# The last 64 rows of the query projection as row pairs, six tiles to a PSUM bank

## The chip, the cores and the metric

The kernel runs on one core of a Trainium2 chip. The metric is the device time of one execution in microseconds, the median of several. TensorE (PE in the profile) multiplies; VectorE (DVE) and ScalarE (ACT) move its results from PSUM to SBUF and do the softmax; GpSimd (POOL) and SyncE (SP) do little here.

## The reference

Four layers, each added to its input: a recurrent memory attention A, a gated unit B, and both once more with the same weights. A goes through 64 segments of 32 tokens one after the other. Each takes 8 memory rows from the segment before.

```python
for s in range(n_seg):                      # 64 segments of 32 tokens
    h = jnp.concatenate([mem, xs], axis=1)  # 8 + 32 rows of 448
    q, k, v = h @ Wq, h @ Wk, h @ Wv        # 16 heads of 256
    p = _softmax(where(mask, q @ k.T * scale, -1e9))
    o = (p @ v) @ Wo
    mem = o[:, :M, :].copy()
    outs.append(o[:, M:, :])
# B: h = relu(x @ W_gate) * (x @ W_up); h @ W_down, with F = 1792
```

(Einsums are written as products here.) Both layers see their input after a layer norm.

## The kernel before

**Fused weights.** For each head the kernel multiplies Wq with the transposed Wk once, at the start (`fuse_qk`), and Wv with Wo (`fuse_vo`). A head is then one 448 x 448 matrix each, in `A_sb` and `B_sb`. The query projection of a step is h times the matrices in `A_sb`, and its result goes straight against h.

**Dimensions.** 448 is three blocks of 128 and one of 64. In `A_sb` the index kd = 0 to 3 is the block of contracted rows; for kd = 3 only the lower 64 rows hold data, and the upper 64 are zero (the memset at line 135). The columns of 16 heads make 2 halves (hf) of 28 tiles of 128 (`NT`): 24 whole tiles, and 4 in which the last 64 columns of two heads stand together.

**Two chains.** The two A layers run interleaved, the second four segments behind the first (`LAG`), so that 60 of the 68 steps work on two segments at once: 2 x 40 = 80 moving columns. The 8 steps at the ends have one chain and 40 columns. Every second step also carries a block of 64 rows of each layer's B (`Feed`: residual, norm, xposed, gate_up, down, norm2, feed_on, leave).

**A step** issues, on TensorE in exactly the order of the program (`in_order`):
- `project`: for each group u of 4 tiles, 16 matmuls `prj` into one bank of PSUM, then a cast to `TQ` by DVE or ACT in turn (the group 6 goes to `TZ` by both). For the first half the groups 6, 0 to 5, then `hk_make` (transposes `kps`), then the same for the second half
- `scores_m(0)`, in between the groups of the second half: the memory scores `Sm`, and on DVE and ACT their softmax (mx, se, ssum, rs, PM)
- behind the projection `flipped(PM[0])` (transposes `pps`), `scores_x` (`Sx`), `weigh_m` (`ya`, `yb`), `scores_m(1)` and `scores_x(1)`
- `project_out` (`ox`), with the gated unit (`ups`, `gps`, `dps`) between its parts in every second step, `project_tail` (`o`), `weigh_m_rows` (`ym`) and `weigh_x` (`y`); the last of these, the weighting of the second half, ends the step

The order on DVE and ACT is set when the program is built. All results of TensorE but `ox` take turns in seven PSUM buffers (pool `psum`). A matmul can use 64 rows of the array alone; `gate_up` issues such matmuls in turn for the lower rows (`ups`) and the upper ones (`gps`). `weigh_x` and `weigh_m_rows` do so with 40 rows.

The code of before, with the profile's line numbers:

Of the kernel before, what the change touches and what calls it, by code (L numbers as in the profile page):

```python
# [8 lines left out]
BF = mybir.dt.bfloat16  # L9
# [43 lines left out]
def build_kernel(ctx, tc, A_x, A_mem0, A_Wq, A_Wk, A_Wv, A_Wo, B_W_gate, B_W_up, B_W_down, out,  # L53
# [26 lines left out]
    def mm(*a, **k):  # L80
        in_order(nc.tensor.matmul(*a, **k))  # L81
# [4 lines left out]
    def evac(eng, dst, src):  # L86
        if eng is nc.scalar:
            nc.scalar.copy(dst, src)  # L88
        else:
            eng.tensor_copy(dst, src)  # L90
# [40 lines left out]
    half = glob.tile([P, 1], F32, name="half")  # L131
    nc.vector.memset(half[:], -0.5)

    A_sb = glob.tile([P, 4, 2, NT, 128], BF, name="A_sb")
    nc.gpsimd.memset(A_sb[ROWS[1], 3], 0.0)
    B_sb = glob.tile([P, 2, NT, DM], BF, name="B_sb")

    hTb = []
# [57 lines left out]
    with tc.tile_pool(name="pre", bufs=3) as pre:  # L196
# [37 lines left out]
        def dims(t, r, e, c, n=1):  # L234
            o = 64 * c if r == 0 else DM + 64 * ((c + 1) % NPASS)
            return t[:, e, o:o + 64 * n]

        def halves(dst, lhs, rhs):
            for t in range(2):
                for eo in range(2):  # L240
                    mm(dst[ROWS[eo]], lhs(eo, 2 * eo + t), rhs(2 * eo + t), start=(t == 0), stop=(t == 1),
                       tile_position=(0, 64 * eo))

        def fuse_qk(p, qk):
            hf, p4 = divmod(p, 4)
            mx_ps = psum.tile([P, 4, 128], F32, tag="ps", name="mxw")
            for kd in range(4):
                rows = slice(0, P if kd < 3 else 64)
                for eo in range(2):
                    aps = psum.tile([P, 3, 128], F32, tag="ps", name="aps")  # L250
                    for t in range(2):
                        e = 2 * eo + t
                        mm(aps[:, :, :], qk[:, e, kd * 128:kd * 128 + 128], dims(qk, 1, e, 0, 6),
                           start=(t == 0), stop=(t == 1))
                    for t in range(2):
                        e = 2 * eo + t
                        mm(mx_ps[:, kd, eo * 64:eo * 64 + 64], qk[:, e, kd * 128:kd * 128 + 128], dims(qk, 1, e, 6),
                           start=(t == 0), stop=(t == 1))
                    evac(nc.scalar if eo or kd == 2 else nc.vector,
                         A_sb[rows, kd, hf, eo * 4 + p4:eo * 4 + p4 + 17:8, :], aps[rows])  # L260
            evac(nc.vector, A_sb[:, 0:3, hf, 24 + p4, :], mx_ps[:, 0:3])
            evac(nc.scalar, A_sb[ROWS[0], 3, hf, 24 + p4, :], mx_ps[ROWS[0], 3])

        def fuse_vo(p, vv, wo):
            hf, p4 = divmod(p, 4)
# [110 lines left out]
    class Feed:  # L376


        def __init__(self, i):
            self.i = i  # L380
            self.first = i < nblk
            self.second = 0 <= i - LAG // BLK < nblk
            self.n = slice(0 if self.second else TB, P if self.first else TB)
            self.x = xa[i % 3]
            self.nx = xp[i % 2]
# [60 lines left out]
                rows_in(nc.scalar, self.i + 2, 0, tps[:, :, 0:TB])  # L446


    def moving(hb, j, idx, chains):

        if len(chains) == 2:
            return hb[:, j, idx * HI:(idx + 1) * HI].rearrange("p (c k) -> p c k", k=64)[:, :, 0:L]
        c = chains[0]
        return hb[:, j, idx * HI + 64 * c:idx * HI + 64 * c + L]

    def project(hf, chains, hb, j, us):

        n = L * len(chains)
        for u in us:
            ps = psum.tile([P, 512], F32, tag="ps", name="prj")  # L460
            for p4 in range(4):
                for kd in range(4):
                    mm(ps[:, p4 * n:(p4 + 1) * n], A_sb[:, kd, hf, 4 * u + p4, :],
                       moving(hb, j, kd, chains), start=(kd == 0), stop=(kd == 3))
            if u < 6:
                parts = [(nc.scalar if u % 2 else nc.vector, slice(0, P), TQ[hf][:, :, u, :])]
            else:
                parts = [(nc.vector, slice(0, 64), TZ[hf][0:64, :, 0:64]),
                         (nc.scalar, slice(64, 128), TZ[hf][64:128, :, 64:128])]
            for eng, rows, T in parts:  # L470
                T = T.rearrange("p g (t q) -> p t g q", q=16)
                if len(chains) == 2:
                    evac(eng, T, ps[rows, 0:4 * n].rearrange("p (t g q) -> p t g q", t=4, q=16))
                    continue
                c = chains[0]
                src = ps[rows, 0:4 * n].rearrange("p (t w) -> p t w", t=4)
                x, m = (0, SEG) if c == 0 else (MEM, 0)
                evac(eng, T[:, :, 2, MEM * c:MEM * c + MEM], src[:, :, m:m + MEM])
                evac(eng, T[:, :, 3 * c:3 * c + 2, :],
                     src[:, :, x:x + SEG].rearrange("p t (g q) -> p t g q", q=16))  # L480

    def queries(hf, g, kd):
        return TQ[hf][:, g, 2 * kd:2 * kd + 2, :] if kd < 3 else TZ[hf][:, g, :]
# [49 lines left out]
    def step(g, ff):  # L533
# [12 lines left out]
        def hk_make():  # L546
            kps = psum.tile([P, 4, 128], BF, tag="ps", name="kps")
            for i in range(4):
                tr(kps[:, i, :], hb[:, j, i * HI:(i + 1) * HI], ident[:])
            hk = HK[g % 2]  # L550
            nc.vector.tensor_copy(hk[:, 0:4, :], kps[:])
            nc.scalar.copy(hk[:].rearrange("p k n -> p (k n)")[:, 512:768].rearrange("p (a b) -> p a b", b=64)[:, 0::3, :],
                           kps[:, 3, :].rearrange("p (a b) -> p a b", b=64))
            return hk

        def scores_m(hf):
            if not ms:
                return
            Sp = psum.tile([P, 2, L], F32, tag="ps", name="Sm")
            for kd in range(4):  # L560
                mm(Sp[:, :, :], queries(hf, 2, kd), moving(hb, j, kd, (0, 1)), start=(kd == 0), stop=(kd == 3))
            weights_of(Sp, 2, PM[hf], blk[:], f"m{hf}")

        def scores_x(hf):
            Sp = psum.tile([P, 4, L], F32, tag="ps", name="Sx")
            mm(Sp[:, :, :], ident[:], maskS[:], start=True, stop=False, skip_group_check=True)
            for half in range(2):
                for c in chains:
                    for kd in range(4):
                        mm(Sp[:, 2 * half + c, :], queries(hf, 3 * c + half, kd), moving(hb, j, kd, (c,)),  # L570
                           start=False, stop=(half == 1 and c == chains[-1] and kd == 3), skip_group_check=True)
            return Sp
# [4 lines left out]
        def weigh_m(hf, hk, PT):  # L577
            if not ms:
                return
            ya = psum.tile([P, 256], F32, tag="ps", name="ya")  # L580
            for kd in range(2):
                mm(ya[:, kd * 128:kd * 128 + 128], hk[:, kd, :], PT[:], start=True, stop=True)
            nc.vector.tensor_copy(ys(hf)[:, 0:16, M0:M0 + 16], ya[:].rearrange("p (t q) -> p t q", q=16))  # L583
            yb = psum.tile([P, 192], F32, tag="ps", name="yb")
            mm(yb[:, 0:128], hk[:, 2, :], PT[:], start=True, stop=True)
            for eo in range(2):
                mm(yb[:, 128:192], hk[:, 4 + eo, :], PT[:, 64 * eo:64 * eo + 64], start=(eo == 0), stop=(eo == 1))
            nc.scalar.copy(ys(hf)[:, 16:28, M0:M0 + 16], yb[:].rearrange("p (t q) -> p t q", q=16))
# [89 lines left out]
        def load_some():  # L678
            if g < 3:
                for part in (2 * at[0], 2 * at[0] + 1):  # L680
                    if part < NPASS + FT // 2:
                        load_ff(part)
                at[0] += 1
# [6 lines left out]
            return  # L690

        load_some()
        project(0, chains, hb, j, (6, 0, 1))
        if ff is not None:
            ff.residual()
        project(0, chains, hb, j, (2, 3, 4, 5))
        load_some()
        hk = hk_make()
        if ff is not None:
            ff.norm()  # L700
        project(1, chains, hb, j, (6, 0, 1))
        scores_m(0)
        project(1, chains, hb, j, (2, 3))
        if ff is not None:
            ff.xposed()
        project(1, chains, hb, j, (4, 5))
        if len(chains) == 2:
            pm = flipped(PM[0], 1, "m0")
            Sx0 = scores_x(0)
            weigh_m(0, hk, pm)  # L710
            scores_m(1)
            Sx1 = scores_x(1)
            probs_x(0, Sx0)
        else:
            Sx0 = scores_x(0)
            scores_m(1)
            Sx1 = scores_x(1)
            pm = flipped(PM[0], 1, "m0")
            weigh_m(0, hk, pm)
            probs_x(0, Sx0)  # L720
# [117 lines left out]
```

## Time and profile before

| what | us |
|---|---|
| median of 3 runs (lowest, highest) | 1646.31 (1643.99, 1646.62) |
| the profiled execution | 1647.19 |
| its span in the profile | 1645.4 |
| PE busy / DVE busy / ACT busy in the span | 1614.9 / 1195.1 / 757.6 |
| matmuls prj, 80 columns: count in the trace, busy | 13440, 520.3 |
| casts TQ of 320 elements on DVE: count, busy | 360, 174.2 |
| casts TQ of 320 elements on ACT: count, busy | 360, 153.1 |

A matmul's duration in the profile (about 0.2 us) is that from its issue to its last result; the next one starts much earlier, so the pace is read from one start to the next. Matmuls and weight loads are recorded under line 81, transposes under line 84, copies by ACT under line 88 and by DVE under line 90, since helpers there issue them; the tile's name tells them apart. The granted clock of TensorE is 1.00 in the steps with two chains.

### The profile page before, as it was taken

How to read it: one execution, taken by the hardware profiler on the slowest of the kernel's cores; microseconds unless marked ns; L12 is line 12 of the kernel's file. 1: busy time of each engine (PE TensorE's matmuls, PEld its weight loads, DVE VectorE, ACT ScalarE, POOL GpSimd, SP SyncE). 2: the span in 40 equal slices, each digit the busy share in tenths (PEclk: the TensorE clock that was granted, in tenths of full speed). 3: DMA queues.
4: the chain of work that ended last, by engine and by line, in shares of the span. 5: the costliest groups of instructions: out<-in, count | busy, mean ns of one | idle time of the engine just before them, and what ended most of it. 6: DMA issues, size and time to landing. Idle time of an engine off the chain costs nothing.

```text
span 1645.4 us, 96970 instructions
## 1 busy us (share of the span) xinstructions
PE 1614.9 (98%) x44476; PEld 1495.1 (91%) x44476; DVE 1195.1 (73%) x4095; ACT 757.6 (46%) x2315; POOL 76.7 (5%) x157
## 2 busy tenths in 40 slices
PE   8999999999999999999999999999999999999997
PEld 7688899999999999999999999999999999999985
DVE  7866777777777777777777777777777777777772
ACT  5634444544444444544444444544444444544441
POOL 3100000000000000000000000000000000000000
PEclk9989999999999999999999999999999999999997
DMA  9430000000000000000000000000000000000000
GB/s 267 129 95 8 8 10 8 6 9 9 9 10 10 9 10 8 5 9 9 10 9 9 9 10 8 6 9 9 10 9 10 10 9 8 5 8 6 7 7 6
DMA packets 29465, 33.06 MB, mean 20 GB/s; under 512 B 3320, under 2 KB 28160, under 8 KB 29056
## 3 DMA queue, kind: packets, MB, share of 16 engines
q1 hardware_dynamic: 28992, 26.85, 6.2%
q8 instruction: 348, 5.70, 1.5%
q14 instruction: 61, 0.50, 0.1%
q0 software_dynamic: 64, 0.01, 0.0%
HBM read 23.18 MB, written 1.84 MB: 15 GB/s over the span
## 4 chain that ended last, share of the span: by engine, by line
PE 91%; DVE 5%; ACT 3%; issue 1%; DMA 0%; POOL 0%; POOLq 0%; DVEq 0%; ACTq 0%
PE prj L81 29%; PE ox L81 24%; PE ups L81 10%; PE dps L81 6%; PE o L81 5%; PE y L81 4%; PE Sx L81 3%; ACT xT L401 2%; PE aps L81 1%; PE bps L81 1%; PE Sm L81 1%; DVE TQ L90 1%; PE tpw L84 1%; PE gps L81 1%; PE pps L84 1%; PE kps L84 1%
## 5 line engine op out<-in xcount | busy, mean ns | idle before, releaser
L81 PE MATMUL prj<-hT,A_sb 128*128 128x80 bf16 (+1 forms) x15232 | 571.0, 199 | 0.2
L81 PEld LDWEIGHTS <-A_sb 128*128 128x128 bf16 x15232 | 546.3, 100 | 15.0 <-issue 8.0
L81 PEld LDWEIGHTS <-B_sb 128*128 128x128 bf16 (+1 forms) x15456 | 497.6, 103 | 27.5 <-issue 19.8
L88 ACT CAST TQ<-prj 128x320 bf16<-128x320 f32 (+1 forms) x456 | 170.4, 384 | 120.3 <-PE prj L81 114.3
L81 PE MATMUL ox<-Y,B_sb 128*128 128x80 bf16 (+4 forms) x5880 | 223.2, 199 | 1.9 <-DVE Y L583 1.9
L81 PE MATMUL ox<-Z,B_sb 128*128 128x80 bf16 (+2 forms) x5712 | 217.9, 199 | 1.3 <-DVE Z L583 1.3
L90 DVE CAST TQ<-prj 128x320 bf16<-128x320 f32 (+1 forms) x456 | 192.6, 430 | 29.2 <-PE prj L81 22.2
L81 PE MATMUL gps<-xT,Wgu_sb 64*128 64x128 bf16 (+1 forms) x3332 | 192.8, 215 | 2.6 <-issue 2.4
L81 PE MATMUL ups<-xT,Wgu_sb 64*128 64x128 bf16 (+1 forms) x3332 | 192.8, 215 | 2.2 <-issue 1.3
L81 PEld LDWEIGHTS <-Wgu_sb 64*128 64x128 bf16 x6664 | 180.9, 95 | 7.7 <-issue 5.6
L415 DVE SCALAR_TENSOR_TENSOR hh<-gps,ut 128x256 bf16<-128x256 f32 (+1 forms) x238 | 96.8, 407 | 58.4 <-ACT ut L414 45.8
L414 ACT CAST ut<-ups 128x256 bf16<-128x256 f32 (+1 forms) x238 | 85.6, 360 | 87.5 <-PE gps L81 69.8
L494 ACT ACTIVATE se<-se 128x80 f32<-128x80 f32 (+1 forms) x270 | 74.9, 299 | 105.2 <-DVE se L493 81.3
L88 ACT CAST Y<-y 64x128 bf16<-64x128 f32 (+2 forms) x256 | 89.3, 379 | 45.7 <-DVE Y L90 42.0
L90 DVE CAST Y<-y 64x128 bf16<-64x128 f32 (+2 forms) x256 | 102.1, 419 | 10.9 <-ACT Y L88 2.0
L512 DVE COPY PT<-pps 128x128 bf16<-128x128 bf16 (+1 forms) x206 | 49.8, 256 | 81.0 <-PE pps L84 76.0
L90 DVE CAST Z<-y 64x128 bf16<-64x128 f32 (+2 forms) x256 | 99.1, 418 | 10.2 <-ACT Z L88 3.4
L88 ACT COPY hT<-tps 128x256 bf16<-128x256 bf16 x32 | 11.9, 372 | 195.5 <-DVE hT L90 195.5
L88 ACT CAST Z<-y 64x128 bf16<-64x128 f32 (+2 forms) x256 | 89.2, 378 | 24.0 <-DVE Z L90 17.4
L81 PE MATMUL dps<-Wd_sb,hh 128*128 128x448 bf16 x476 | 98.5, 360 | 0.0
L81 PEld LDWEIGHTS <-TQ 128*128 128x128 bf16 x1938 | 88.3, 97 | 11.2 <-ACT TQ L88 10.8
L88 ACT CAST TZ<-prj 64x320 bf16<-64x320 f32 (+2 forms) x152 | 56.0, 378 | 71.7 <-DVE TZ L90 71.2
(121 smaller groups left out, 2075.6 us busy)
## 6 DMA issues: line engine op xcount, KB each, us to landing
wo<-in_A_Wo_dram SPq DMA_DIRECT2D x8, 448.0 KB, 7.8
nat<-in_A_Wq_dram SPq DMA_DIRECT2D x8, 384.0 KB, 6.0
nat<-in_A_Wk_dram SPq DMA_DIRECT2D x8, 384.0 KB, 6.1
nat<-in_A_Wv_dram SPq DMA_DIRECT2D x8, 384.0 KB, 7.8
xa<-in_A_x_dram SPq DMA_DIRECT2D x32, 56.0 KB, 2.2
xa<-xp SPq DMA_DIRECT2D x32, 56.0 KB, 1.9
out_dram<-xa SPq DMA_DIRECT2D x32, 56.0 KB, 2.0
xp<-in_A_x_dram SPq DMA_DIRECT2D x30, 56.0 KB, 2.1
```

The costliest lines, as they stand in the source:

```text
L81: in_order(nc.tensor.matmul(*a, **k))
L84: in_order(nc.tensor.transpose(*a))
L88: nc.scalar.copy(dst, src)
L90: eng.tensor_copy(dst, src)
L401: nc.scalar.copy(xT[ROWS[r], 4:NPASS, :], tps[ROWS[1 - r], 0:3, :])
L414: nc.scalar.copy(ut[:, :, n], ups[:, :, n])
L415: nc.vector.scalar_tensor_tensor(out=hh[:, 2 * u:2 * u + 2, n], in0=gps[:, :, n], scalar=0.0, in1=ut[:, :, n], op0=ALU.max, op1=ALU.mult)
L494: nc.scalar.activation(se[:], se[:], AF.Exp, scale=SCALE)
L512: nc.vector.tensor_copy(PT[:], pps[:].rearrange("p b q -> p (b q)"))
```

## The change

The rows of kd = 3 leave `A_sb` and go to `A3` and `A3z`, each tile in 64 rows, half of the tiles in the lower and half in the upper ones. A tile's projection is now one matmul of 64 rows and three of 128. The banks hold six tiles (four for `TZ`), so a step has four banks and one `TZ` bank for each half. `open_banks` issues the matmuls of 64 rows for two banks in turn, one on the lower rows, one on the upper ones; `close_bank` adds the three others and casts. A step has three such groups: of 6 pairs at its start, of 10 pairs (with the `TZ` banks of both halves), and of 12 pairs for the second half. A cast has 480 elements. `xposed` moves from inside the projection to behind `weigh_m(0)`, and `scores_m(0)` stands behind the first of the four banks of the second half. `fuse_qk` makes the new tiles with matmuls of 64 columns.

```diff
-    A_sb = glob.tile([P, 4, 2, NT, 128], BF, name="A_sb")
-    nc.gpsimd.memset(A_sb[ROWS[1], 3], 0.0)
+    A_sb = glob.tile([P, 3, 2, NT, 128], BF, name="A_sb")
+    A3 = glob.tile([P, 2, 12, 128], BF, name="A3")
+    A3z = glob.tile([P, 4, 128], BF, name="A3z")
...
-            for kd in range(4):
-                rows = slice(0, P if kd < 3 else 64)
+            for kd in range(3):
...
+            aps = psum.tile([P, 3, 128], F32, tag="ps", name="aps")
+            halves(aps, lambda eo, e: qk[:, e, 384:448], lambda e: dims(qk, 1, e, 0, 6))
+            for eo in range(2):
+                for t in range(2):
+                    e = 2 * eo + t
+                    mm(mx_ps[ROWS[hf], 3, eo * 64:eo * 64 + 64], qk[:, e, 384:448], dims(qk, 1, e, 6),
+                       start=(t == 0), stop=(t == 1), tile_position=(0, 64 * hf))
+            evac(nc.scalar, A3[:, hf, p4:p4 + 9:4, :], aps[:])
             evac(nc.vector, A_sb[:, 0:3, hf, 24 + p4, :], mx_ps[:, 0:3])
-            evac(nc.scalar, A_sb[ROWS[0], 3, hf, 24 + p4, :], mx_ps[ROWS[0], 3])
+            evac(nc.scalar, A3z[ROWS[hf], p4, :], mx_ps[ROWS[hf], 3])
...
-    def project(hf, chains, hb, j, us):
+    class Bank:
+        def __init__(self, hf, i):
+            self.hf = hf
+            self.i = i
+            self.tiles = [tidx(kd, i // 2, 2 * (i % 2) + k) for kd in range(3) for k in range(2)] if i < 4 else list(range(24, NT))
+            self.ps = psum.tile([P, 512], F32, tag="ps", name="prj")
...
+    def open_banks(chains, hb, j, *which):
+        n = L * len(chains)
+        banks = [Bank(hf, i) for hf, i in which]
+        for a, b in zip(banks[::2], banks[1::2]):
+            for k in range(len(a.tiles)):
+                for bk in (a, b):
+                    t = bk.tiles[k]
+                    r, w = last_rows(bk.hf, t)
+                    mm(bk.out(t, n), w, moving(hb, j, 3, chains, ROWS[r]), start=(k == 0), stop=False,
+                       skip_group_check=True)
+        return banks
+
+    def close_bank(bk, chains, hb, j, eng):
+        n = L * len(chains)
+        hf, N = bk.hf, len(bk.tiles)
+        for t in bk.tiles:
+            for kd in range(3):
+                mm(bk.out(t, n), A_sb[:, kd, hf, t, :], moving(hb, j, kd, chains), start=False, stop=(kd == 2),
+                   skip_group_check=True)
...
-        project(0, chains, hb, j, (6, 0, 1))
+        b0, b2 = open_banks(chains, hb, j, (0, 0), (0, 2))
+        close_bank(b0, chains, hb, j, nc.vector)
+        close_bank(b2, chains, hb, j, nc.scalar)
         if ff is not None:
             ff.residual()
-        project(0, chains, hb, j, (2, 3, 4, 5))
+        b1, b3, z0, z1 = open_banks(chains, hb, j, (0, 1), (0, 3), (0, 4), (1, 4))
+        close_bank(b1, chains, hb, j, nc.vector)
         load_some()
+        close_bank(b3, chains, hb, j, nc.scalar)
+        close_bank(z0, chains, hb, j, None)
         hk = hk_make()
         if ff is not None:
             ff.norm()
-        project(1, chains, hb, j, (6, 0, 1))
+        close_bank(z1, chains, hb, j, None)
+        c0, c2, c1, c3 = open_banks(chains, hb, j, (1, 0), (1, 2), (1, 1), (1, 3))
+        close_bank(c0, chains, hb, j, nc.vector)
         scores_m(0)
-        project(1, chains, hb, j, (2, 3))
-        if ff is not None:
-            ff.xposed()
-        project(1, chains, hb, j, (4, 5))
+        close_bank(c2, chains, hb, j, nc.scalar)
+        close_bank(c1, chains, hb, j, nc.vector)
+        close_bank(c3, chains, hb, j, nc.scalar)
         if len(chains) == 2:
             pm = flipped(PM[0], 1, "m0")
             Sx0 = scores_x(0)
             weigh_m(0, hk, pm)
+            if ff is not None:
+                ff.xposed()
             scores_m(1)
```

In the steps with one chain `xposed` stands behind `scores_x(0)`.

More of the change, by code (lines that the diff above doesn't have):

```diff
@@ L259, in fuse_qk @@
                     evac(nc.scalar if eo or kd == 2 else nc.vector,
-                         A_sb[rows, kd, hf, eo * 4 + p4:eo * 4 + p4 + 17:8, :], aps[rows])
+                         A_sb[:, kd, hf, eo * 4 + p4:eo * 4 + p4 + 17:8, :], aps[:])
+            aps = psum.tile([P, 3, 128], F32, tag="ps", name="aps")
[6 more added lines that the diff above has]
+            evac(nc.scalar, A3[:, hf, p4:p4 + 9:4, :], aps[:])
             evac(nc.vector, A_sb[:, 0:3, hf, 24 + p4, :], mx_ps[:, 0:3])
-            evac(nc.scalar, A_sb[ROWS[0], 3, hf, 24 + p4, :], mx_ps[ROWS[0], 3])
+            evac(nc.scalar, A3z[ROWS[hf], p4, :], mx_ps[ROWS[hf], 3])
         def fuse_vo(p, vv, wo):
@@ L446, in feed_on, with moving @@
                 rows_in(nc.scalar, self.i + 2, 0, tps[:, :, 0:TB])
-    def moving(hb, j, idx, chains):
+    def moving(hb, j, idx, chains, rows=slice(0, P)):
         if len(chains) == 2:
-            return hb[:, j, idx * HI:(idx + 1) * HI].rearrange("p (c k) -> p c k", k=64)[:, :, 0:L]
+            return hb[rows, j, idx * HI:(idx + 1) * HI].rearrange("p (c k) -> p c k", k=64)[:, :, 0:L]
         c = chains[0]
-        return hb[:, j, idx * HI + 64 * c:idx * HI + 64 * c + L]
-    def project(hf, chains, hb, j, us):
-        n = L * len(chains)
[L459 to L480, printed above, removed]
@@ new lines, in moving, with out @@
+        return hb[rows, j, idx * HI + 64 * c:idx * HI + 64 * c + L]
+    class Bank:
[4 more added lines that the diff above has]
+            self.ps = psum.tile([P, 512], F32, tag="ps", name="prj")
+        def out(self, t, n):
+            k = self.tiles.index(t)
+            return self.ps[:, k * n:(k + 1) * n]
@@ new lines, in last_rows @@
+    def last_rows(hf, t):
+        if t >= 24:
+            return hf, A3z[ROWS[hf], t - 24, :]
+        kd, eo, p4 = t // 8, t // 4 % 2, t % 4
+        return eo, A3[ROWS[eo], hf, 4 * kd + p4, :]
+    def open_banks(chains, hb, j, *which):
+        n = L * len(chains)
+        banks = [Bank(hf, i) for hf, i in which]
[7 more added lines that the diff above has]
+        return banks
@@ new lines, in close_bank @@
+    def close_bank(bk, chains, hb, j, eng):
[5 more added lines that the diff above has]
+                   skip_group_check=True)
+        ps = bk.ps
+        if bk.i < 4:
+            at = 2 * (bk.i // 2) + bk.i % 2
+            parts = [(eng, slice(0, P), TQ[hf][:].rearrange("p g (k b) w -> p g k (b w)", b=2)[:, :, :, 32 * at:32 * at + 32], 3)]
+        else:
+            parts = [(nc.vector, slice(0, 64), TZ[hf][0:64, :, 0:64].unsqueeze(2), 1),
+                     (nc.scalar, slice(64, 128), TZ[hf][64:128, :, 64:128].unsqueeze(2), 1)]
+        for eng, rows, T, K in parts:
+            T = T.rearrange("p g k (t q) -> p k t g q", q=16)
+            if len(chains) == 2:
+                evac(eng, T, ps[rows, 0:N * n].rearrange("p (k t g q) -> p k t g q", k=K, t=N // K, q=16))
+                continue
+            c = chains[0]
+            src = ps[rows, 0:N * n].rearrange("p (k t w) -> p k t w", k=K, t=N // K)
+            x, m = (0, SEG) if c == 0 else (MEM, 0)
+            evac(eng, T[:, :, :, 2, MEM * c:MEM * c + MEM], src[:, :, :, m:m + MEM])
+            evac(eng, T[:, :, :, 3 * c:3 * c + 2, :],
+                 src[:, :, :, x:x + SEG].rearrange("p k t (g q) -> p k t g q", q=16))
@@ L715, in step @@
             Sx0 = scores_x(0)
+            if ff is not None:
+                ff.xposed()
             scores_m(1)
```

## The prediction

> **What bounds the kernel now.** I read the page first, then the groups of instructions kept apart by shape, then the timeline of one step and of TensorE's changes of array shape, last the windows around the few stretches in which the clock fell.
>
> ```profile
> PE 1614.9 (98%) x44476; PEld 1495.1 (91%) x44476; DVE 1195.1 (73%) x4095; ACT 757.6 (46%) x2315; POOL 76.7 (5%) x157
> ...
> PE 91%; DVE 5%; ACT 3%; issue 1%; DMA 0%; POOL 0%; POOLq 0%; DVEq 0%; ACTq 0%
> ```
>
> TensorE (PE) is busy throughout and is 91% of the chain that ended last. So what the change takes from TensorE's stream counts in full, and so does every wait that it puts into it. DMA is 0% of the chain. The chain in order of time prices the projection:
>
> ```profile
> 803.87 2.29 PE prj L81 x64
> ```
>
> 64 matmuls in 2.29 us are 35.8 ns each (128 rows, 80 columns). The 224 of a step cost 8.02 us; 60 of the 68 steps have both chains, thus 80 columns.
>
> Two more prices come from timelines. The first column is the start, the second the time to the end of the last; matmuls overlap, so I go from start to start.
>
> ```profile
> 827.62 0.42 PE L81 MATMUL ox<-Z,B_sb 128*128 128x80 bf16 x7
> 827.96 0.23 PE L81 MATMUL ups<-xT,Wgu_sb 64*128 64x128 bf16 x1
> 827.97 0.23 PE L81 MATMUL gps<-xT,Wgu_sb 64*128 64x128 bf16 x1
> 828.03 0.22 PE L81 MATMUL ups<-xT,Wgu_sb 64*128 64x128 bf16 x1
> ...
> 843.37 0.61 PE L81 MATMUL y<-PT,hk 40*128 40x256 bf16 x8
> 843.91 0.28 PE L81 MATMUL prj<-hT,A_sb 128*128 128x80 bf16 x3
> ```
>
> A row pair exists already: ups (rows 0 to 63) and gps (rows 64 to 127) start 4 ns apart and the next pair 56 ns after the first, as long as one full matmul of 128 columns (the four of kps take 0.22 us). A pair costs one matmul. A change of shape costs more: the last ox starts at 827.83 and the first ups 0.134 us later, where 0.036 would do: 0.098 us. The last y starts at 843.71 and the first prj 0.20 us later where 0.109 would do: 0.093 us. From gps to y (64 to 40 rows) nothing is lost: 52 ns, the pace of the pairs.
>
> **The saving on TensorE.** The change replaces 56 of the 224 matmuls by 28 pairs. At 80 columns a pair should take 35.8 ns; ym's pairs of 64 columns come every 28 ns, so weight loads allow that. Saved: 28 x 35.8 = 1.00 us a step. The first group follows y, which is in row shape already, so it only moves a switch that is paid now. The second and third groups add two switches each, four of about 0.097 us: 0.39 us. Net 0.61 us a step, 36.6 us in 60 steps. The 8 steps with one chain have 40 columns, 25 ns a matmul and 28 a pair: 56 x 25 - 28 x 28 - 390 = 0.2 us, 1.6 us in all. In the fusing of the weights each pair of heads loses four matmuls of 384 columns (162 ns apart) for two column pairs at 162 ns and about 0.2 us of switches: 0.13 us, 1.0 us for eight. POOL's memset of A_sb (6.07 us) and eight DVE casts of 550 ns go as well; both lay beside TensorE's stream there, so I count them at nothing.
>
> **The moved xposed.** In every second step the memory scores of the second half now wait, in the middle of Sm, for ACT's last cast of TQ, which stands behind the two xT copies (473 ns each): 30 such waits of 0.30 us, 9.0 us. With xposed behind weigh_m that cast is early and the wait goes. xT is next needed by the first ups, 1.8 us after its transposes (Sm, Sx and 30 ox lie between); DVE's copy behind ya's (415 + 417 ns), then two ACT copies, end about then, and the rows from ACT are first read 16 matmuls later. I cost this at nothing. Without that cover it is at most the 0.3 us again, 9 us. Residual, norm and xposed issue no DMA; POOL's two small operations for rstd have over a microsecond to spare. The weight pieces queued on SP move by a microsecond in the first three steps, on a queue with no share in the chain.
>
> **The wait that the change makes.** Behind each first memory score stands a softmax chain over DVE and ACT, and then pps, for which TensorE waits in order:
>
> ```profile
> 803.67 0.20 PE L81 MATMUL Sm<-hT,TZ 128*128 128x80 bf16 x1
> ...
> 803.76 0.43 ACT L88 CAST TQ<-prj 128x320 bf16<-128x320 f32 x1 [0.21 <-PE prj L81]
> 803.91 0.24 DVE L491 TENSOR_REDUCE mx<-Sm 128x2 f32<-128x80 f32 x1 [0.23 <-PE Sm L81]
> 804.18 0.24 DVE L493 TENSOR_TENSOR se<-Sm,mx 128x80 f32<-128x80 f32 x1
> 804.46 0.27 ACT L494 ACTIVATE se<-se 128x80 f32<-128x80 f32 x1 [0.27 <-DVE se L493]
> 804.48 0.49 DVE L90 CAST TQ<-prj 128x320 bf16<-128x320 f32 x1
> 804.89 0.23 DVE L500 TENSOR_REDUCE ssum<-se 128x2 f32<-128x80 f32 x1
> 805.05 0.42 ACT L88 CAST TQ<-prj 128x320 bf16<-128x320 f32 x1 [0.33 <-PE prj L81]
> 805.15 0.17 DVE L502 RECIPROCAL rs<-ssum 128x2 f32<-128x2 f32 x1
> 805.35 0.16 DVE L504 TENSOR_TENSOR rs<-rs,blk 128x2 f32<-128x2 f32 x1
> 805.54 0.24 DVE L505 TENSOR_TENSOR PM<-se,rs 128x80 bf16<-128x80 f32 x1
> ...
> 806.00 0.22 PE L84 MATMUL pps<-ident,PM 128*128 128x128 bf16 x1
> ```
>
> PM ends at 805.78 and TensorE reaches pps at 806.00: 0.22 us to spare, under a cover of 64 prj matmuls (2.29 us). The change shortens the cover and lengthens the chain. The cover becomes three banks of 18 matmuls, 1.93 us. And the casts now stand in the chain: the built program has on DVE the cast of c0, mx, se, ssum, the cast of c1, rs, rs, PM, and on ACT the cast of c2 ahead of the exponential. Before, the bank ahead of Sm was cast by ACT, beside mx on DVE.
>
> A cast has 480 elements. DVE takes 484 ns for 320, 624 for 448 and 686 for 512; ACT 425, 532 and 598. Between the last two: 0.65 us and 0.565 us. Let T be the start of c0's last matmul, with the hand-overs of the rows above (0.24 us from a matmul's start to a reader, 0.03 to 0.04 between engines or dependent steps, 0.08 overlap of independent ones). DVE: c0's cast T+0.24 to 0.89; mx to 1.05; se to 1.32. ACT: c2's last matmul starts at 0.79, cast 1.03 to 1.60, exponential to 1.78. DVE: ssum to 2.04; c1's cast 1.96 to 2.61; rs to 2.69; times blk to 2.88; PM to 3.15. pps can start at 3.21, and TensorE is there at T+2.11 (Sm, then 54 matmuls). The wait is **1.10 us**. The same walk put on the rows of before gives PM at T+2.27, and the trace has 2.26. In the steps with the feed forward DVE has also the residual, its statistics and norm; counted the same way it finishes z1's cast 0.2 us before c0's comes, so the wait is the same. Behind the wait sit all of the step's remaining matmuls; DVE and ACT do nothing in it that is wanted later on TensorE, so it isn't given back.
>
> If the cast cost no more than the rows of 320 the wait would be 0.78 us; at the rows of 512, 1.16. I take 1.10, since 448 and 512 enclose it. PSUM's seven buffers add no wait: the tightest, z1 behind the last y casts, has some 0.3 us.
>
> The sum: -36.6 - 1.6 - 1.0 - 9.0 = -48.2; 60 x 1.10 = +66; together +17.8 us on the profiled execution (1647.19 us, its span 1645.4): 1665.0. That execution is 0.9 us above the median of the runs shown, so 1664.
>
> **The rivals.** *The chain keeps up (faster).* If the casts get out of the softmax's way so that PM is late by no more than 0.5 us, the time is 1646.3 - 48.2 + 30 = 1628, and 1598 with no wait at all. For it speaks that the whole gain is bought on the bounding engine. Against it speak the order on DVE and ACT and the walk that fits before to 0.01 us. It decides below a wait of 48.2 / 60 = 0.80 us. *No difference:* casts of 480 at about the price of 320, a wait of 0.78 us: 1645.
>
> *The clock falls.* A wait of 1.1 us leaves TensorE idle about 0.9 us beyond its last matmul.
>
> ```profile
> 82.40:85.90 3.50, 1.97 (x40) 1.47 (x38) 2.72 (x18) 1.43 (x6) 3.38 (x2) 0.94 0.91 212
> 85.90:89.30 3.40, 3.40 (x95) 3.21 (x95) 1.98 (x11) 0.66 (x2) 0.00 (x0) 0.50 0.64 169
> 103.00:106.40 3.40, 2.45 (x83) 2.23 (x80) 3.18 (x17) 1.15 (x4) 0.00 (x0) 1.00 0.31 76
> ```
>
> The second column is TensorE's busy time, the third from the end the granted clock. 1.97 of 3.50 us was followed by half clock; 2.45 of 3.40 was not. 0.9 us idle is on the good side, but not by much. A stretch of 3.4 us at half speed loses 1.7 us; after every second wait that is 51 us: 1715. The Trainium skill, "TensorE: Matmul & The Clock Gate", section "A second HAM failure mode: psum-queue depth-cycling", says that frequent micro-idling between groups of matmuls can make the clock oscillate; by that rule the 1715 would be the forecast. This trace speaks against it so far, by the last row.
>
> *The pairs don't overlap*, as when two accumulations into different banks hindered each other: 28 x 35.8 ns more in 60 steps, 60 us: 1724. ups and gps accumulate just so, and they overlap.
>
> **How the numbers follow.** The forecast, slower with a wait of 0.85 to 1.35 us, has 0.70 (1649 to 1680; late xT copies could add some). The chain keeps up: 0.15. No difference: 0.07. Clock: 0.05. Pairs: 0.03. Runs of this kernel tell about 0.2% (3.3 us) from no change. Faster 0.15, same 0.07, slower 0.78. The range leaves out the better half of the faster case and the two dear ones: 1630 to 1690.
>
> **What would show it.** Right: pps behind c3 waits for DVE's PM about 1.1 us, with casts of 128x480 at 0.65 (DVE) and 0.565 us (ACT) in between; 28 pairs 36 ns apart; four more changes of shape near 0.1 us; no wait inside Sm; the clock at 1.00. Wrong: pps without idle time ahead of it, or the wait elsewhere, in a bank that isn't free or in ups behind xT.

## The result and the profile after

| kernel | median us (lowest, highest) | ratio to before, 95% interval |
|---|---|---|
| before, runs beside the changed kernel | 1645.15 (1643.24, 1646.62) | |
| changed | 1663.86 (1661.85, 1664.00) | 1.0112 [1.0094, 1.0129] |

The changed kernel is 1.1% slower. Its profiled execution took 1663.9 us with a span of 1662.1 us, 16.7 us more than before. The page of the changed kernel, engines and chain:

```profile
PE 1580.9 (95%) x44476; PEld 1448.8 (87%) x44476; DVE 1163.5 (70%) x3935; ACT 730.4 (44%) x2163; POOL 70.7 (4%) x156
...
PE 88%; DVE 7%; ACT 3%; issue 1%; DMA 0%; SPq 0%; POOL 0%; POOLq 0%; ACTq 0%; DVEq 0%
```

TensorE is busy for 34.0 us less (1614.9 before) in a span that is 16.7 us longer, and DVE's part of the chain went from 5 to 7%: time was taken out of TensorE's stream and more was put in as waiting. All three other engines are busy for less than before, too. None of them became a bound by its load; a sequence of short steps did.

The timeline of a step with two chains, around the first memory scores (the columns are start, length to the end of the last, engine, line, operation, shapes; in brackets the idle time before it and who ended it):

```profile
812.34 0.20 PE L81 MATMUL Sm<-hT,TZ 128*128 128x80 bf16 x1
812.38 2.10 PE L81 MATMUL prj<-hT,A_sb 128*128 128x80 bf16 x54
812.44 0.66 DVE L90 CAST TQ<-prj 128x480 bf16<-128x480 f32 x1 [0.73 <-PE prj L81]
813.01 0.23 DVE L533 TENSOR_REDUCE mx<-Sm 128x2 f32<-128x80 f32 x1
813.22 0.56 ACT L88 CAST TQ<-prj 128x480 bf16<-128x480 f32 x1 [1.05 <-PE prj L81]
813.28 0.24 DVE L535 TENSOR_TENSOR se<-Sm,mx 128x80 f32<-128x80 f32 x1
813.68 0.27 ACT L536 ACTIVATE se<-se 128x80 f32<-128x80 f32 x1
813.98 0.24 DVE L542 TENSOR_REDUCE ssum<-se 128x2 f32<-128x80 f32 x1 [0.47 <-ACT se L536]
814.14 0.65 DVE L90 CAST TQ<-prj 128x480 bf16<-128x480 f32 x1
...
815.09 0.24 DVE L547 TENSOR_TENSOR PM<-se,rs 128x80 bf16<-128x80 f32 x1
815.39 0.23 PE L84 MATMUL pps<-ident,PM 128*128 128x128 bf16 x1 [0.91 <-DVE PM L547]
```

Read it from the bottom. pps waited for PM, and the bracket says 0.91 us. That counts from the modelled end of the matmul before it; from its start, 814.28, it is 1.11 us where 0.036 would do. PM was late because c1's cast (814.14) stood between ssum and rs; ssum was late because the exponential began only when c2's cast left ACT (813.22 to 813.78); and mx, ready at 812.58, began at 813.01 behind c0's cast. Counted over the 60 steps with two chains, the wait is 1.10 us on average (1.07 us in steps without the feed forward, 1.13 us with it): 66 us. Measured from the start of the first half's last `Sm` matmul, PM ends after 2.12 us in the steps of before without the feed forward, and after 2.99 us here; TensorE's last `prj` starts after 2.29 and 1.94 us. The chain is thus 0.87 us longer and its cover 0.36 us shorter. The kernel before had 0.15 us to spare, beyond the 0.06 us from PM's end to pps: 0.87 + 0.36 - 0.15 = 1.08.

The groups of the changed kernel give the casts and the pairs:

```profile
L90 DVE CAST TQ<-prj 128x480 bf16<-128x480 f32 x240 | 156.3, 651 | 50.5 <-PE prj L81 48.7
L88 ACT CAST TQ<-prj 128x480 bf16<-128x480 f32 x240 | 134.2, 559 | 181.7 <-PE prj L81 181.7
L81 PE MATMUL prj<-hT,A 64*128 64x80 bf16 x2880 | 82.3, 199 | 0.0
```

The group of pairs behind the weighting, on TensorE:

```profile
805.94 0.61 PE L81 MATMUL y<-PT,hk 40*128 40x256 bf16 x8
806.39 0.38 PE L81 MATMUL prj<-hT,A 64*128 64x80 bf16 x12
806.70 0.39 PE L81 MATMUL prj<-hT,A_sb 128*128 128x80 bf16 x6
```

The last y starts at 806.28 and the first pair 0.106 us later, the plain pace of y: no switch is paid there. Twelve matmuls start within 0.18 us (0.38 less the 0.20 of the last), two every 36 ns. The next full matmul comes 0.131 us after the last of them: the switch that used to stand behind y.

### The profile page after: what moved, and what is told of

Its sections match the earlier page's. It is cut to its first block, busy times and chain, and to the rows that moved or that the text cites. A ratio compares the mean times of both kernels' runs of the same rounds, so it can differ in the third digit from the quotient of the medians.

```text
span 1662.1 us, 96485 instructions
## 1 busy us (share of the span) xinstructions
PE 1580.9 (95%) x44476; PEld 1448.8 (87%) x44476; DVE 1163.5 (70%) x3935; ACT 730.4 (44%) x2163; POOL 70.7 (4%) x156
## 4 chain that ended last, share of the span: by engine, by line
PE 88%; DVE 7%; ACT 3%; issue 1%; DMA 0%; SPq 0%; POOL 0%; POOLq 0%; ACTq 0%; DVEq 0%
PE prj L81 25%; PE ox L81 24%; PE ups L81 10%; PE dps L81 6%; PE o L81 5%; PE y L81 4%; PE Sx L81 3%; DVE TQ L90 2%; PE pps L84 2%; ACT TQ L88 2%; PE bps L81 1%; PE aps L81 1%; DVE ssum L542 1%; PE tpw L84 1%; PE Sm L81 1%
## 5 line engine op out<-in xcount | busy, mean ns | idle before, releaser
L81 PE MATMUL prj<-hT,A_sb 128*128 128x80 bf16 (+1 forms) x11424 | 452.0, 200 | 0.1
L81 PEld LDWEIGHTS <-A_sb 128*128 128x128 bf16 x11424 | 415.1, 100 | 12.7 <-issue 0.3
L88 ACT CAST TQ<-prj 128x480 bf16<-128x480 f32 (+2 forms) x304 | 147.7, 497 | 198.5 <-PE prj L81 198.1
L90 DVE CAST TQ<-prj 128x480 bf16<-128x480 f32 (+2 forms) x304 | 171.7, 572 | 56.6 <-PE prj L81 53.7
L542 DVE TENSOR_REDUCE ssum<-se 128x2 f32<-128x80 f32 (+1 forms) x270 | 70.9, 274 | 39.8 <-ACT se L536 37.3
L81 PE MATMUL prj<-hT,A 64*128 64x80 bf16 (+1 forms) x3264 | 94.0, 197 | 0.0
```

Of the source, the lines that this page charges most:

```text
L542: nc.vector.tensor_reduce(ssum[:], se[:], axis=AX.X, op=ALU.add)
```

## The experiments

My theory is that the wait of pps is all that is lost, and that casts in front of and inside the softmax chain, together with the shorter cover, make it. The rivals are that pairs or switches cost more than assumed, or that the wait comes from the cover alone. All kernels ran beside the kernel before.

**The scores ahead of c0's matmuls.** The edit to the changed kernel:

```diff
         c0, c2, c1, c3 = open_banks(chains, hb, j, (1, 0), (1, 2), (1, 1), (1, 3))
-        close_bank(c0, chains, hb, j, nc.vector)
         scores_m(0)
+        close_bank(c0, chains, hb, j, nc.vector)
```

> One edit to the changed kernel: the first memory scores stand ahead of bank c0's three full matmuls a tile, not behind them. The softmax chain then has four banks (72 matmuls, 2.58 us) as cover and c0's cast no longer stands in front of it. Theory (the whole loss is the wait of pps for PM, 1.10 us in 60 steps = 66 us): the wait goes entirely and nothing takes its place, 1663.9 - 66 = 1598 us, within 1592 to 1608. Rival 1 (pairs, switches or larger casts themselves cost more than they save): the place of the scores matters little, 1650 to 1664. Rival 2 (the wait only moves: Sm then waits for z0's cast on ACT, or pps still waits behind c0's cast): 1610 to 1640.

Measured: 1593.33 us (1592.37 to 1594.69), 0.9684 [0.967, 0.9699] of before: 3.2% faster than before, and 70.5 us less than the changed kernel. Its timeline:

```profile
824.39 0.20 PE L81 MATMUL Sm<-hT,TZ 128*128 128x80 bf16 x1
824.43 2.75 PE L81 MATMUL prj<-hT,A_sb 128*128 128x80 bf16 x72
824.45 0.42 ACT L88 CAST TZ<-prj 64x320 bf16<-64x320 f32 x1
824.63 0.24 DVE L533 TENSOR_REDUCE mx<-Sm 128x2 f32<-128x80 f32 x1 [0.23 <-PE Sm L81]
824.91 0.24 DVE L535 TENSOR_TENSOR se<-Sm,mx 128x80 f32<-128x80 f32 x1
825.18 0.27 ACT L536 ACTIVATE se<-se 128x80 f32<-128x80 f32 x1 [0.32 <-DVE se L535]
825.28 0.66 DVE L90 CAST TQ<-prj 128x480 bf16<-128x480 f32 x1
...
826.51 0.24 DVE L547 TENSOR_TENSOR PM<-se,rs 128x80 bf16<-128x80 f32 x1
826.67 0.65 DVE L90 CAST TQ<-prj 128x480 bf16<-128x480 f32 x1
827.01 0.22 PE L84 MATMUL pps<-ident,PM 128*128 128x128 bf16 x1
```

mx now begins 0.24 us behind the last score, the exponential finds ACT free, and PM ends at 826.75, 0.26 us before TensorE comes for it. pps starts 36 ns after the matmul before it in all 60 steps, and no other wait took the place: 60 x 1.10 = 66 us of the 70.5 are this wait. A step without the feed forward takes 18.12 us (18.68 before, 19.19 in the changed kernel), one with it 26.76 us (27.63 and 27.90). Both rivals fall: pairs, switches and large casts are all still in this kernel.

**The casts on the other engine.** The edit:

```diff
-        close_bank(c0, chains, hb, j, nc.vector)
+        close_bank(c0, chains, hb, j, nc.scalar)
...
-        close_bank(c2, chains, hb, j, nc.scalar)
-        close_bank(c1, chains, hb, j, nc.vector)
-        close_bank(c3, chains, hb, j, nc.scalar)
+        close_bank(c2, chains, hb, j, nc.vector)
+        close_bank(c1, chains, hb, j, nc.scalar)
+        close_bank(c3, chains, hb, j, nc.vector)
```

> One edit to the changed kernel: the casts of the second half's banks change engine (c0 and c1 to ACT, c2 and c3 to DVE). The order on TensorE and the cover of 54 matmuls stay. By the walk of the prediction with the built order (DVE: mx, se, cast of c2, ssum, rs, rs, PM; ACT: cast of c0, exponential, cast of c1) PM ends 2.48 us behind the start of c0's last matmul, not 3.15, so the wait of pps falls from 1.10 to about 0.43 us; the cast of c3 on DVE then delays PT by about 0.2 us, so that ya waits. Theory (the casts in the chain make the wait): 60 x 0.5 = 30 us less, 1634 us, within 1622 to 1645. Rival (the wait comes from the shorter cover alone, the chain being as long as before): no change, 1660 to 1667.

Measured: 1638.62 us, 0.9964 [0.995, 0.9979]. The cover and TensorE's order are those of the changed kernel, and 25 us are gone. The wait of pps is 0.44 us and the new wait of ya 0.16 us, close to what the walk gave; what it had not seen is a wait of 0.27 us in the steps with the feed forward, where the `ups` behind the transposes `ppr` starts 0.31 us after them and not 0.04 (8 us in all). In the timeline c2's cast sits inside the chain instead of c0's and c1's:

```profile
846.77 0.24 DVE L533 TENSOR_REDUCE mx<-Sm 128x2 f32<-128x80 f32 x1 [0.87 <-PE Sm L81]
847.05 0.24 DVE L535 TENSOR_TENSOR se<-Sm,mx 128x80 f32<-128x80 f32 x1
847.33 0.27 ACT L536 ACTIVATE se<-se 128x80 f32<-128x80 f32 x1
847.42 0.66 DVE L90 CAST TQ<-prj 128x480 bf16<-128x480 f32 x1
848.00 0.23 DVE L542 TENSOR_REDUCE ssum<-se 128x2 f32<-128x80 f32 x1
...
848.95 0.23 PE L84 MATMUL pps<-ident,PM 128*128 128x128 bf16 x1 [0.28 <-DVE PM L547]
```

ssum could have begun at 847.64, 0.04 us behind the exponential's end, and waited 0.36 us for that cast. With the cover unchanged, the engines of the casts are worth 0.66 of the 1.10 us. This also prices the cover: from the start of the first half's last `Sm` to the end of PM it is 2.36 us both here and with the scores ahead, so the chain is equally long, and the 18 more matmuls of cover there (0.64 us) are what turns a wait of 0.44 us into none.

**A fourth group.** The edit:

```diff
-        c0, c2, c1, c3 = open_banks(chains, hb, j, (1, 0), (1, 2), (1, 1), (1, 3))
+        c0, c2 = open_banks(chains, hb, j, (1, 0), (1, 2))
         close_bank(c0, chains, hb, j, nc.vector)
         scores_m(0)
         close_bank(c2, chains, hb, j, nc.scalar)
+        c1, c3 = open_banks(chains, hb, j, (1, 1), (1, 3))
```

> One edit to the changed kernel: the third group is split, and the pairs of c1 and c3 are issued behind c2's matmuls. This adds two changes of shape a step (0.195 us) and puts them and six pairs (0.215 us) under the wait of pps; in the built order the softmax also comes ahead of c1's cast on DVE. Theory: TensorE's stream is 0.195 us longer, yet the wait falls from 1.10 to about 0.25 us, with up to 0.25 us of a new wait of ya for PT behind c1's cast: 1625 to 1645 us. Rival (what costs time in the changed kernel is the switching): 60 x 0.195 = 12 us more, 1676 us.

Measured: 1630.40 us (1628.73 to 1633.46), 0.9911 [0.9893, 0.9929]. Two more switches a step, and it is 33 us faster than the changed kernel: the wait of pps is 0.24 us, that of ya 0.16 us. The switches and the six pairs lie under what was a wait, and a step with two chains is still 0.52 us shorter on average. The longer cover and the order of c1's cast behind the softmax came together; the trace shows what each gave in the steps without the feed forward: PM ends 2.55 us behind the start of the first half's last `Sm`, not 2.99, and the last `prj` starts after 2.36 us, not 1.94.

**The order within a group.** The edit:

```diff
-            for k in range(len(a.tiles)):
-                for bk in (a, b):
+            for bk in (a, b):
+                for k in range(len(a.tiles)):
```

> One edit to the changed kernel: within a group all 64-row matmuls of one bank go before those of the other, so that lower and upper rows no longer alternate; the number of instructions and of switches is the same. Theory (a pair costs as much as one matmul, 35.8 ns): 28 x 35.8 ns = 1.00 us more in each of 60 steps and about 0.6 us in the 8 others, 1664 + 65 = 1729 us. Rival (the pairs save little or overlap in either order): 1664 to 1680 us.

Measured: 1679.83 us, 1.0209 [1.0188, 1.023]: 16 us more than the changed kernel, not 65, and the theory's number was wrong. The group behind the weighting:

```profile
831.48 0.47 PE L81 MATMUL prj<-hT,A 64*128 64x80 bf16 x12
831.88 0.25 PE L81 MATMUL prj<-hT,A_sb 128*128 128x80 bf16 x2
```

Twelve starts spread over 0.27 us instead of 0.18; one after the other at 36 ns they would need 0.39. Sorted by time, the starts of such a group fit two rows of six, each 35 to 41 ns apart, the second beginning 0.083 us after the first, when three of the first six have started. The trace does not name the array rows of a matmul. But started strictly in the order of the program, the first six, all on the same rows, would lie within 0.12 us; the next run shows that six on the same rows need 0.18. So some matmuls on the upper rows ran ahead of lower ones that stand earlier in the program. Each group costs about 0.085 us more, three of them in 60 steps 15 us, close to the 16 measured. So the run did not price the pairs, and the next was made for it.

**All on the lower rows.** The edit (half of the tiles thereby get another tile's last rows):

```diff
         if t >= 24:
-            return hf, A3z[ROWS[hf], t - 24, :]
+            return 0, A3z[ROWS[0], t - 24, :]
         kd, eo, p4 = t // 8, t // 4 % 2, t % 4
-        return eo, A3[ROWS[eo], hf, 4 * kd + p4, :]
+        return 0, A3[ROWS[0], hf, 4 * kd + p4, :]
```

> The changed kernel with all 64-row matmuls on the lower 64 rows (half of the tiles thereby use another tile's weights for their last rows; counts, shapes, banks and switches are the same). In the run with the order changed, lower and upper rows still overlapped, so that it did not price the pairs; here no two can. Theory: each 64-row matmul then costs 35.8 ns like a full one, 28 x 35.8 ns = 1.00 us more in 60 steps and about 0.5 us in the 8 others: 1664 + 64 = 1728 us, 1715 to 1735. Rival (64-row matmuls are cheap by themselves, not by their overlap): 1664 to 1690 us.

Measured: 1726.24 us, 1.0488 [1.0469, 1.0507], 62 us more than the changed kernel. The group of twelve (the last start 0.59 - 0.20 = 0.39 us behind the first, 36 ns each):

```profile
856.28 0.59 PE L81 MATMUL prj<-hT,A 64*128 64x80 bf16 x12
856.81 0.32 PE L81 MATMUL prj<-hT,A_sb 128*128 128x80 bf16 x4
```

A matmul of 64 rows costs as much as one of 128. The gain comes from the overlap alone, and it is the 1.00 us a step of the sum: the 60 steps with two chains take 60.4 us more than in the changed kernel. The wait of pps is unchanged at 1.10 us here.

**xposed alone.** The edit to the kernel before:

```diff
-        if ff is not None:
-            ff.xposed()
         project(1, chains, hb, j, (4, 5))
...
             weigh_m(0, hk, pm)
+            if ff is not None:
+                ff.xposed()
             scores_m(1)
```

(in steps with one chain, behind `scores_x(0)`)

> The kernel before with one part of the change alone: xposed stands behind weigh_m of the first half, not inside the projection. Theory (the 30 waits of 0.30 us inside Sm come from ACT's xT copies ahead of the last cast of TQ): 9 us less than before, 1637 us, ratio 0.9945. Rival (the xT copies are then late for the first ups, which waits in turn): 1643 to 1650 us, ratio 0.998 to 1.002.

Measured: 1634.97 us beside 1645.42 of before, 0.9932 [0.9919, 0.9946]: 10.4 us less. The timeline of before has the wait inside Sm, that of this run has not:

```profile
825.88 0.57 PE L81 MATMUL Sm<-hT,TQ 128*128 128x80 bf16 x3
826.28 0.21 PE L81 MATMUL Sm<-hT,TZ 128*128 128x80 bf16 x1
```

```profile
867.38 0.27 PE L81 MATMUL Sm<-hT,TQ 128*128 128x80 bf16 x3
867.49 0.20 PE L81 MATMUL Sm<-hT,TZ 128*128 128x80 bf16 x1
```

Three Sm matmuls take 0.57 us in the one and 0.27 us in the other. A step with the feed forward goes from 27.63 to 27.34 us, 0.29 us in each of 30 steps, 8.8 us. The other 1.6 us cannot be put down to the edit: the two profiled executions differ by 4.1 us in the eight steps with one chain, 2.9 of it in the last, where the granted clock stood at 0.50 for 17 us before and for 10 us here. The first ups does not wait.

## Why the prediction was right, step by step

- **The wait of pps**, forecast at 1.10 us from a walk along the queues, is 1.10 us. The casts that it rested on, 0.65 and 0.565 us by the rows of 448 and 512 elements, are 0.651 and 0.559 us. That the wait is the same with the feed forward was off by 0.05 us: ACT's cast of c2 begins that much later in those steps, and why is not shown.
- **The pairs** come every 36 ns as forecast; the run on the lower rows confirms the 1.00 us. (The pairs of `ups` and `gps`, from which this was argued, come every 55 ns by their starts, 3 ns apart; only the first one takes 65 ns.)
- **The switches**: 0.134 us into a group and 0.131 us out, 0.098 and 0.099 more than the pace (0.036 from pair to pair, 0.032 from a pair's second matmul). The first group pays none.
- **The net on TensorE** was 0.61 us a step. Steps without the feed forward and without the wait (the scores ahead) are 0.56 us shorter than before. The size was 0.05 us too large, 3 us in all. About 0.03 us of it lies within the groups: their starts spread over 0.184, 0.334 and 0.405 us, where 35.8 ns a pair would give 0.179, 0.322 and 0.394. Where the rest goes is open.
- **The moved xposed**: 9.0 us forecast; alone it took 8.8 us out of the 60 steps (10.4 by the medians).
- **The parts beside the 60 steps** were mis-sized. I gave them -2.6 us. The 60 steps took 23.0 us more by the trace, and the span grew by 16.7, so the setup and the ends gave back about 6.3. Of these, 1.6 us lie before the first prj and 4.7 in the eight steps with one chain. 3.2 of the 4.7 are in the last step, where the granted clock stood at 0.50 for 17 us before and for 10 us after, so that they need not come from the change. The start of the first prj varies too: 73.0 to 74.8 us in the six kernels with the new setup, 76.2 and 76.4 us in the two with the old. The forecast of 20.4 for the 60 steps and -2.6 beside them was thus 3 us low and 4 us high. That the total came out within a microsecond is luck.
- **The clock** stayed at 1.00 through all steps with two chains, though the wait comes once in each. A window of the changed kernel around one wait:

```profile
812.00:815.42 3.42, 2.51 (x71) 2.38 (x68) 2.32 (x8) 1.46 (x4) 0.00 (x0) 1.00 0.02 5
```

TensorE is busy for 2.51 of 3.42 us, as in the window of before that kept full clock (2.45 of 3.40). The Trainium skill, "TensorE: Matmul & The Clock Gate", section "A second HAM failure mode: psum-queue depth-cycling", says that frequent micro-idling between groups of matmuls made the clock oscillate in a kernel; the trace of the changed kernel shows none of it, with one wait of 1.1 us a step and the granted clock at 1.00.

- **The other rivals**: that the chain keeps up came true only in the run with the scores one line higher, 1593.33 us where that rival gave 1598 with no wait at all. That the pairs don't overlap was wrong.

## What to carry to other kernels

When work is taken out of the bounding engine, look for what that work was covering: here 1.00 us of pairs a step was bought and 1.10 us of wait came with it, from 10 fewer matmuls behind Sm and larger casts in the queues of its softmax. Price such a chain by walking the two queues in their built order, casts included, and compare with the cover that is left. The remedy was to issue the start of the chain as soon as its inputs exist, ahead of the next bank's matmuls.

## What was not expected of the hardware

Matmuls on the lower and upper 64 rows of the array need not alternate in the program to overlap: with six on the one and then six on the other, the second row of starts began 0.083 us after the first, before the first six had all started, and the starts of the group of twelve spread over 0.27 us, against 0.18 alternating and 0.39 on the same rows.
